# Two read-back loads moved up in a DMA queue and the last output store divided, in a gated FFT-filter kernel

## The chip, the core and the metric

The kernel runs on one core of a Trainium2 chip. A core has a matrix engine (PE, whose weight loads are listed apart as PEld), a vector engine (DVE), a scalar engine (ACT), a general engine (POOL) and a queue engine (SP) that does no arithmetic and issues the transfers; the transfers themselves run on the core's 16 DMA engines. The metric is the device time of one execution in microseconds (us); lower is better. The kernel before takes 117.5 us (median of 11 runs).

## What is computed

One input `x` of shape (1, 2048, 1024) goes through two Fourier filters that differ only in their weights, and the two results are mixed row by row with a gate:

```python
g = sigmoid((x * gate_w).sum(-1, keepdims=True))
def filt(x, w_r, w_i):
    X = rfft2(x.astype(float32), axes=(-2, -1)) * (w_r + 1j * w_i)
    return irfft2(X, s=(2048, 1024), axes=(-2, -1)).astype(bfloat16)
a, b = filt(x, A_w_r, A_w_i), filt(x, B_w_r, B_w_i)
return g * a + (1 - g) * b          # 2048 x 1024, bfloat16
```

## The kernel before, in words

The transforms are matrix products with cosine and sine tables. Columns of the spectrum are split into an even and an odd half (called parity 0 and 1); rows are split as 2048 = 128 x 16. The forward half of the kernel (tokens `F1`, `F2`, `F3`) brings the input to the spectrum, DVE multiplies the spectrum with both sets of weights (`P`, L494), and the first inverse stage (`J`, L537) works on 16 blocks: blocks 0 to 7 are the even parity, 8 to 15 the odd one.

Between the first inverse stage and the last two, the data changes its layout by a round trip through DRAM. A block's result is copied from PSUM to an `rl` tile (`R`, L204 on ACT or L206 on DVE), and two stores of 256 KB a block carry it to a scratch tensor `sc` (`H:block:half`, L549). Once all stores of a parity are there, eight loads of 512 KB bring it back (`L:parity:pair`, L554), the even parity into the tile `re` and the odd one into `ro`; a *pair* is two of the 16 row groups. Every load of a parity reads from all of its stores, so the first odd load `L:1:0` cannot be issued before the last odd store `H:15:0` has landed. Stores and loads are all issued by SP, in one queue. The kernel was given eight semaphores for the transfers of that queue, taken in turn, so each transfer is issued only when the eighth one before it has landed.

From the loaded pair PE computes the second inverse stage (`V:parity:pair:s`, L565: eight 128x128 products, s is the row of the pair), ACT or DVE copies the result to a `V` tile, and PE computes the last stage: `C` for the even parity (L590), `U` (L581) or `C` for the odd one. Even results are kept in `re` as sums and differences (`EX` copies them from PSUM, `EQ` on POOL, L615, adds and subtracts; `E` is a direct copy). Odd results are combined with the even ones into the output tile `ot` of the pair: `OR:pair:s:h` on DVE straight from PSUM (L635; h = 0 is the sum and the first half row, h = 1 the difference and the second half row), `OP` on POOL (L631) from a copy `OC`, and `QD` on DVE with `QP` on POOL (L642, L647) for pair 3. `S:S:pair` or `S:S:pair:s` stores both rows or one row of a finished pair (L652); a row in `ot` is 1024 elements of bfloat16, so a pair's tile is 512 KB and a row of it 256 KB. `ot` tiles share their five buffers with `rl` tiles.

The order of all this is written by hand: the string `ORDER` is a list of tokens, each token calls one function of `gated_mix`, and the instructions stand on every engine in just this order. No scheduler moves them. The last token of `V`, `C`, `U`, `F1` and so on is the PSUM bank; a letter A, D, P or S is the engine.

Around the change the even loads stand like this in `ORDER`: `L:0:0` to `L:0:4` early, then `L:0:5` after the stores `H:12:0` and `H:10:1`, then the nine stores `H:11:0`, `H:13:0`, `H:11:1`, `H:12:1`, `H:14:1`, `H:13:1`, `H:14:0`, `H:15:1`, `H:15:0`, then `L:0:6`, `L:0:7`, and then the odd loads `L:1:0` to `L:1:7`. PE uses them in the order of the tokens: `V:0:6` and `V:0:7` after the even pair 5, and `V:1:0` after them. The work ends with pair 6: four `OR` of it on DVE, of which the last three are the last three instructions of DVE, and one store `S:S:6` of the whole pair.

Of the kernel before, what the change touches and what calls it, by code (L numbers as in the profile page):

```python
# [10 lines left out]
P = 128  # L11
S = 2048
D = 1024
# [8 lines left out]


ORDER = """
warm:8 c:A:F1 c:A:gws tab:A x:S:0:1 x:S:1:1 x:S:2:2 x:S:4:2 x:S:6:2 x:S:8:2 x:S:10:2 x:S:12:2 x:S:14:2 c:S:FD:0:1
F1:1:o:0 F1:1:e:1 FX:1:o:D F1:0:o:2 FC:1:e:D F1:0:e:3 FP:1:o FD:1:e F1:3:o:0 F1:2:e:4 FC:0:e:D F1:3:e:1 gc:P FD:0:e
F1:2:o:5 FC:3:e:A FC:2:e:D F1:4:e:3 FD:3:e FX:2:o:A F1:5:o:6 FX:0:o:A FD:2:e F1:5:e:5 FC:4:e:A FP:0:o FX:3:o:A FD:4:e
F1:6:e:1 FC:5:e:A F1:4:o:2 FD:5:e FC:6:e:A F1:7:e:0 FP:2:o c:S:WF:0:4 FD:6:e F1:6:o:3 W:S:0 FC:7:e:A F1:9:e:7 FD:7:e
FX:6:o:A F1:8:e:1 FP:3:o FC:9:e:D c:S:WJ:0:4 F1:11:e:3 FD:9:e F1:10:e:0 c:S:w0 FC:11:e:A F1:7:o:4 c:S:PM FC:8:e:A
FP:6:o FD:11:e FX:5:o:A c:S:EZ F1:13:e:5 FC:10:e:A FD:8:e W:S:1 F1:12:e:6 FP:5:o FD:10:e c:S:WF:4:16 FC:12:e:A  # L30
F1:14:e:1 FC:13:e:A FD:12:e FX:4:o:A F1:15:e:3 W:S:2 F1:15:o:0 FD:13:e FP:4:o FC:15:e:A F1:11:o:2 FC:14:e:A FD:15:e
FC:15:o:A F1:8:o:6 c:S:WJ:4:16 F1:14:o:5 FD:14:e FC:8:o:A F1:10:o:3 neg:A:0:4 FD:15:o FC:14:o:A F1:12:o:7 FX:7:o:A
F2:0:0:1 FD:8:o c:S:E FC:10:o:A FP:7:o FC:12:o:A F2:1:0:0 W:S:3 FD:14:o T:0:0:A F2:0:1:4 FC:11:o:A F2:1:1:6 FD:10:o
T:1:0:A W:S:4 pw:P F1:13:o:1 T:1:1:A FD:12:o F1:9:o:0 T:0:1:A F3:1:5 FD:11:o c:S:FD:1:2 FC:9:o:A F3:0:3 FC:13:o:A
FD:9:o X:1:A W:S:5 F2:3:1:2 FD:13:o F2:2:0:7 X:0:A F2:3:0:0 P:1:0 W:S:6 Y:1:1 F2:2:1:5 T:3:0:A Y:0:3 neg:A:4:16 GH:4
P:1:1 W:S:7 T:2:0:A T:2:1:A NA:1:D N:1:D P:0:0 T:3:1:A GC:A NA:0:D P:0:1 F3:2:0 F2:4:0:5 X:2:A F2:4:1:2 F3:3:6 J:1:3:0
T:4:0:D T:4:1:A X:3:A P:2:0 Y:2:2 GT:0:5 R:1:0:A F2:5:0:6 Y:3:7 NA:2:D P:2:1 T:5:0:A H:1:0 F3:4:2 c:S:IG R:1:1:A
GT:1:5 W:S:8 F2:5:1:4 N:0:D NA:3:D P:3:0 X:4:A J:0:6:0 W:S:9 T:5:1:A H:1:1 N:2:D GT:2:5 P:3:1 R:0:0:A Y:4:2 GT:3:5
F3:5:3 W:S:10 R:0:1:A N:3:D H:0:0 F2:7:1:6 GK:D NA:4:D P:4:0 F2:6:1:2 X:5:A GZ:0:0 F2:6:0:5 P:4:1 GS:0 W:S:11 F2:7:0:7
T:7:0:A T:7:1:D J:2:3:0 T:6:0:A GW:D:4 T:6:1:A Y:5:6 GW:D:0 R:2:0:A N:4:D NA:5:D P:5:0 R:2:1:A H:2:0 W:S:12 H:0:1  # L40
P:5:1 F3:7:6 J:3:2:4 X:7:A H:2:1 F3:6:0 R:3:0:A F2:8:0:6 X:6:D F2:8:1:7 R:3:1:A F2:9:0:2 Y:7:3 T:8:0:D Y:6:0 T:8:1:A
GZ:1:4 NA:6:D T:9:0:A P:7:0 J:4:6:0 GS:1 F2:9:1:2 N:5:D P:7:1 R:4:0:A T:9:1:A H:4:0 P:6:0 J:5:4:6 W:S:13 R:4:1:A H:3:0
NA:7:D N:7:D R:5:0:A H:4:1 P:6:1 F3:8:2 F3:9:0 R:5:1:A F2:11:1:4 X:8:D F2:10:0:5 X:9:A H:5:1 F2:10:1:6 H:3:1 N:6:D
F2:11:0:7 W:S:14 P:8:0 T:10:0:A J:6:2:0 T:11:0:A T:11:1:A T:10:1:D R:6:0:A P:8:1 J:7:4:6 R:6:1:A H:6:0 F3:10:2 H:5:0
P:9:0 R:7:0:A P:9:1 R:7:1:A H:7:0 J:8:0:4 X:10:A GW:D:12 H:7:1 F2:12:0:6 H:6:1 F2:12:1:7 W:S:15 R:8:0:A T:12:0:D
P:10:0 R:8:1:A J:9:2:0 P:10:1 T:12:1:A H:8:1 F3:11:4 H:8:0 R:9:0:A F2:13:1:6 X:11:D R:9:1:A H:9:0 F3:12:2 F2:14:0:7
X:12:A H:9:1 F2:13:0:0 L:0:0 F2:14:1:1 L:0:1 T:13:0:A T:13:1:D P:11:0 L:0:2 J:10:4:2 L:0:3 T:14:0:A P:11:1 T:14:1:A
F3:13:6 R:10:0:A P:12:0 X:13:A H:10:0 J:11:0:4 L:0:4 P:12:1 R:10:1:A F3:14:6 R:11:0:A X:14:D F2:15:0:2 F2:15:1:3
T:15:0:A P:13:0 T:15:1:A J:12:0:6 R:11:1:A V:0:0:1:2 P:13:1 R:12:0:A F3:15:4 V:0:0:0:3 R:12:1:D X:15:A H:12:0
V:0:1:0:0 H:10:1 V:0:1:1:1 L:0:5 VC:0:1:0:A P:14:0 H:11:0 J:13:4:6 VC:0:0:0:A VC:0:1:1:A P:14:1 VC:0:0:1:A R:13:0:A  # L50
P:15:0 J:14:0:2 R:13:1:A H:13:0 H:11:1 C:0:0:1:4 P:15:1 H:12:1 C:0:0:0:5 EX:0:0:D R:14:0:D R:14:1:A EX:0:1:A H:14:1
J:15:6:2 H:13:1 EQ:0:1:0:P V:0:2:0:4 EQ:0:0:0:P C:0:1:1:5 R:15:0:D R:15:1:A H:14:0 C:0:1:0:0 EQ:0:0:1:P H:15:1
V:0:2:1:1 VC:0:2:0:A GW:D:8 V:0:3:1:2 H:15:0 EX:1:1:A L:0:6 V:0:3:0:3 VC:0:2:1:A EX:1:0:D L:0:7 EQ:1:1:0:P C:0:2:0:4
VC:0:3:0:D VC:0:3:1:A C:0:2:1:1 EQ:1:0:0:P V:0:4:1:0 EX:2:1:D EQ:0:1:1:P V:0:4:0:5 C:0:3:0:2 EQ:2:1:0:P VC:0:4:0:A
C:0:3:1:1 EX:2:0:A V:0:5:0:3 EQ:1:1:1:P VC:0:4:1:A V:0:5:1:5 EQ:1:0:1:P VC:0:5:0:A C:0:4:0:4 VC:0:5:1:A EQ:2:0:0:P
L:1:0 C:0:5:0:0 EX:4:0:D L:1:1 C:0:4:1:3 L:1:2 E:3:0:D EQ:4:0:0:P L:1:3 V:0:6:0:5 EX:4:1:A L:1:4 C:0:5:1:4 L:1:5
EQ:2:0:1:P VC:0:6:0:D V:0:6:1:2 L:1:6 EX:5:0:D EQ:4:0:1:P V:0:7:1:3 VC:0:6:1:A V:0:7:0:5 EX:5:1:A EQ:5:0:0:P C:0:6:0:0
L:1:7 C:0:6:1:2 EQ:2:1:1:P EX:6:1:A EQ:5:1:0:P VC:0:7:0:A VC:0:7:1:D E:3:1:D C:0:7:1:3 V:1:0:0:1 V:1:0:1:4 EQ:4:1:0:P
VC:1:0:0:A C:0:7:0:2 VC:1:0:1:D EX:6:0:A EQ:6:1:0:P U:1:0:0:1 EX:7:0:A EQ:6:1:1:P V:1:1:0:0 OC:0:0:A EQ:5:0:1:P
V:1:1:1:2 VC:1:1:0:D U:1:0:1:4 EQ:6:0:0:P V:1:2:0:5 EQ:7:0:0:P V:1:2:1:0 VC:1:2:0:A EQ:7:0:1:P U:1:1:0:1 VC:1:2:1:D  # L60
VC:1:1:1:A EQ:4:1:1:P EX:7:1:A U:1:2:0:5 OP:0:0:0 OR:0:1:1 OC:1:0:A OR:0:1:0 U:1:1:1:0 OR:2:0:0 EQ:6:0:1:P V:1:3:0:1
U:1:2:1:4 OP:0:0:1 VC:1:3:0:A V:1:3:1:2 V:1:4:0:1 OP:1:0:0 OR:1:1:0 OR:2:0:1 OR:2:1:1 S:S:0 VC:1:3:1:A OR:1:1:1
C:1:3:0:3 VC:1:4:0:A V:1:4:1:5 OR:2:1:0 EQ:7:1:0:P C:1:3:1:0 VC:1:4:1:A QD:3:0:0 S:S:2 U:1:4:0:1 OP:1:0:1 QD:3:1:1
V:1:5:0:2 QD:3:1:0 OC:4:0:A V:1:5:1:4 EQ:5:1:1:P S:S:1 VC:1:5:0:A QD:3:0:1 U:1:4:1:5 OP:4:0:0 VC:1:5:1:D U:1:5:0:0
OR:4:1:0 OP:4:0:1 U:1:5:1:1 OR:5:0:0 OR:4:1:1 V:1:7:0:4 QP:3:0:0:P V:1:6:1:2 OR:5:0:1 S:S:4 VC:1:7:0:A V:1:7:1:3
OR:5:1:1 U:1:7:0:4 VC:1:7:1:A EQ:7:1:1:P OR:5:1:0 V:1:6:0:0 QP:3:1:1:P OR:7:0:0 S:S:5 U:1:7:1:1 VC:1:6:0:A OR:7:0:1
VC:1:6:1:A QP:3:1:0:P U:1:6:0:0 S:S:7:0 OR:7:1:1 OR:7:1:0 U:1:6:1:2 QP:3:0:1:P OR:6:0:0 S:S:7:1 OR:6:1:1 OR:6:0:1
S:S:3 OR:6:1:0 S:S:6
"""


# [115 lines left out]
def gated_mix(ctx, tc, x_in, we_in, wo_in, w0_in, gw_in, out):  # L187
# [4 lines left out]
    ov = out.flatten_outer_dims().rearrange("(s2 s1) d -> s2 s1 d", s1=NS1)  # L192
# [7 lines left out]
    Q = {"S": nc.sync, "P": nc.gpsimd, "A": nc.scalar, "D": nc.vector}  # L200
# [19 lines left out]
    x = Re[:].rearrange("p (s d) -> p s d", s=NS1)  # L220
# [6 lines left out]
    C = {}  # L227
# [7 lines left out]
    warm = C["EA"][:].rearrange("p a b -> p (a b)")[:, 0:512]  # L235
    C["w0"] = C["EB"][:].rearrange("p a b -> p (a b)")[:, 1152:1408].rearrange("p (s u r t a w) -> p s u r t a w", s=2, u=NU, r=2, t=2, a=2)
    cnt = [0, 0]
    Ts, Xs, Ps, RLs, Vs, Ws, PS, TM, OT = {}, {}, {}, {}, {}, {}, {}, {}, {}
# [407 lines left out]
        t = TM["Q", v][:, h].rearrange("p s (g d) -> p s g d", g=2)  # L646
        Q[e].tensor_tensor(otile(v)[:, :, h, 256 * g:256 * g + 256], t[:, :, 0], t[:, :, 1], (ALU.add, ALU.subtract)[g])  # L647

    def store(q, v, s="b"):
        v = int(v)  # L650
        r = slice(0, 2) if s == "b" else slice(int(s), int(s) + 1)
        Q[q].dma_start(ov[:, 2 * v:2 * v + 2, :][:, r], OT[v][:, r].rearrange("p s h d -> p s (h d)"))  # L652

    fn = dict(warm=warmup, x=load_x, c=load_c, W=load_w, neg=neg, gc=gate_coef, tab=table, pw=pair_weights,
              F1=f1, FG=f1g, FY=f1y, FC=f1c, FD=f1d, FX=f1x, FP=f1p, GH=gate_hat, GC=gate_copy, GT=gate_turn, GK=gate_cols, GZ=gate_z, GS=gate_s, GW=gate_weights,
              F2=f2, T=f2c, F3=f3, X=f3c, P=prod, Y=parts, NA=patch_mul, N=patch, J=i1, R=i1c, H=scratch_store, L=scratch_load, V=i2, VC=i2c, U=i3, C=i3f,
              E=even_out, ES=even_sin, EF=even_sum, EX=even_parts, EQ=even_mix, OC=odd_copy, OP=odd_pool, OR=odd_row, QD=odd_mix, QP=odd_out, S=store)
    order = [tok.split(":") for tok in ORDER.split()]
    for t in order:
# [53 lines left out]
```

## Time and profile before

| what | value |
|---|---|
| median of 11 runs (lowest to highest) | 117.5 us (117.11 to 118.22) |
| the profiled execution's own time | 115.97 us |
| its span, first to last instruction | 114.2 us |
| PE busy | 102.7 us (90%) |
| DVE busy | 96.9 us (85%) |
| ACT busy | 84.5 us (74%) |
| POOL busy | 46.2 us (40%) |
| moved by DMA over the span | 36.79 MB, mean 322 GB/s |
| granted PE clock, mean | 0.995 of full speed |

Times inside the profile count from the first instruction of the span. "SPq" is SP issuing a transfer: the time beside it is that of the issue, not of the transfer, whose landing is given separately as time from issue to landing. In the chain of waits each piece was released by the piece before it; "issue" is time in which nothing that the profile shows was waited for. Because one execution is profiled, a difference of time is read inside it and then added to the median.

### The profile page before, as it was taken

Reading aid. Unit: us, or ns where it says so; the run is one execution under the profiler, and the core shown is the slowest. Engines: PE = TensorE matmul, PEld = TensorE weight load, DVE = VectorE, ACT = ScalarE, POOL = GpSimd, SP = SyncE. Lnnn points to the kernel's source line nnn. Section 1 sums busy time; section 2 is a strip of 40 time slices with the busy share of each in tenths; the row PEclk is TensorE's granted clock in tenths of the full one; section 3 lists DMA queues with packets and bytes.
Section 4 is the critical chain, followed back from the end, with each engine's and each line's share of the span. In section 5 each row is a group of like instructions: output and inputs, shape, how many; then the busy total and the mean of one; then the engine's idle time right before and its main releaser. Section 6 shows DMA issues by size and latency. Waiting matters only on the chain.

```text
span 114.2 us, 3953 instructions
## 1 busy us (share of the span) xinstructions
PE 102.7 (90%) x1619; PEld 70.7 (62%) x1619; DVE 96.9 (85%) x164; ACT 84.5 (74%) x138; POOL 46.2 (40%) x74
## 2 busy tenths in 40 slices
PE   5999999999999699897889899989999999999900
PEld 2599889775567356473445457459979666857400
DVE  0199999999999999999899999999266449999970
ACT  4018678999999999999999999977646753534300
POOL 1087994900000000000000000047988999999910
PEclk9999999999999999999999999999999999999998
DMA  3999999999488999579999999999999996583874
GB/s 92 369 354 413 396 363 369 353 412 420 189 253 292 362 397 396 165 223 395 377 330 370 302 349 394 290 366 381 351 354 321 354 416 245 225 326 135 323 277 184
DMA packets 17794, 36.79 MB, mean 322 GB/s; under 512 B 1904, under 2 KB 10736, under 8 KB 17776
## 3 DMA queue, kind: packets, MB, share of 16 engines
q1 hardware_dynamic: 17488, 36.44, 88.3%
q8 instruction: 12, 0.20, 0.7%
q10 hardware_dynamic: 288, 0.10, 0.5%
q14 instruction: 6, 0.05, 0.1%
HBM read 23.96 MB, written 12.58 MB: 320 GB/s over the span
## 4 chain that ended last, share of the span: by engine, by line
PE 33%; DMA 25%; DVE 18%; ACT 13%; issue 6%; SPq 1%; DVEq 1%; ACTq 0%
DMA re<-in_x_dram 9%; PE ps L581 9%; DVE p L494 9%; ACT rl L204 8%; PE ps L565 8%; DMA re<-sc 5%; DMA sc<-rl 4%; PE ps L334 4%; PE ps L450 4%; DMA ig<-cst_ig 4%; DMA gws<-in_gw_dram 3%; ACT X L204 3%; PE ps L590 3%; ACT T L204 2%; DVE ot L635 2%
## 5 line engine op out<-in xcount | busy, mean ns | idle before, releaser
L615 POOL TENSOR_TENSOR re<-wx 128x256 f32<-128x256 f32 x28 | 19.6, 730 | 54.7 <-DMA sc<-rl 53.2
L204 ACT CAST rl<-ps 128x1024 bf16<-128x1024 f32 x29 | 29.7, 1145 | 0.7 <-PE ps L537 0.7
L204 ACT COPY wx<-ps 128x256 f32<-128x256 f32 (+1 forms) x39 | 17.2, 500 | 9.7 <-PE ps L334 6.7
L537 PE MATMUL ps<-p,wj 32*64 32x512 bf16 x512 | 20.5, 381 | 2.5 <-ACT rl L204 2.0
L204 ACT CAST V<-ps 128x512 bf16<-128x512 f32 x25 | 13.8, 603 | 10.6 <-PE ps L565 7.7
L494 DVE TENSOR_TENSOR p<-X,ro 128x2048 bf16<-128x2048 bf16 x16 | 19.2, 1218 | 0.0
L450 PE MATMUL ps<-fd,y 128*128 128x256 bf16 x128 | 16.5, 273 | 0.5 <-ACT rl L204 0.4
L382 DVE TENSOR_TENSOR y<-ps,wx 128x256 bf16<-128x256 f32 x48 | 16.5, 420 | 0.1
L334 PE MATMUL ps<-f,re 128*128 128x128 bf16 x256 | 15.3, 219 | 0.5 <-DMA re<-in_x_dram 0.5
L204 ACT CAST T<-ps 128x512 bf16<-128x512 f32 x26 | 15.5, 696 | 0.0
L334 PEld LDWEIGHTS <-re 128*128 128x128 bf16 x256 | 14.5, 98 | 1.6 <-DMA re<-in_x_dram 1.2
L537 PEld LDWEIGHTS <-wj 32*64 32x64 bf16 x512 | 8.4, 103 | 10.7 <-issue 7.5
L382 POOL TENSOR_TENSOR y<-wx 128x256 bf16<-128x256 f32 x16 | 11.1, 729 | 7.4 <-DVE wx L206 5.2
L635 DVE TENSOR_TENSOR ot<-re,ps 128x512 bf16<-128x512 f32 x22 | 13.8, 682 | 0.4
L450 PEld LDWEIGHTS <-y 128*128 128x128 bf16 x128 | 11.6, 97 | 4.1 <-issue 2.8
L581 PE MATMUL ps<-ig,V 128*128 128x512 bf16 x56 | 13.4, 379 | 0.0
L204 ACT CAST X<-ps 128x1024 bf16<-128x1024 f32 x12 | 13.2, 1121 | 0.0
L206 DVE COPY wx<-ps 128x512 f32<-128x512 f32 (+1 forms) x10 | 5.7, 579 | 6.7 <-PE ps L334 4.2
L480 PE MATMUL ps<-T,wf 64*64 64x256 bf16 (+1 forms) x128 | 10.2, 332 | 1.1 <-DVE np L514 0.9
L590 PE MATMUL ps<-ig,V 128*128 128x256 bf16 x72 | 9.7, 273 | 0.0
L494 DVE TENSOR_TENSOR p<-X,wx 128x2048 bf16<-128x2048 bf16 x8 | 9.4, 1218 | 0.0
L494 DVE TENSOR_TENSOR p<-X,y 128x2048 bf16<-128x2048 bf16 x8 | 9.3, 1220 | 0.0
(60 smaller groups left out, 138.1 us busy)
## 6 DMA issues: line engine op xcount, KB each, us to landing
sc<-rl SPq DMA_DIRECT2D x32, 256.0 KB, 4.9
ro<-in_we_dram SPq DMA_DIRECT2D x8, 512.0 KB, 7.7
re<-sc SPq DMA_DIRECT2D x8, 512.0 KB, 6.0
ro<-sc SPq DMA_DIRECT2D x8, 512.0 KB, 7.2
re<-in_x_dram SPq DMA_DIRECT2D x7, 512.0 KB, 7.6
out_dram<-ot SPq DMA_DIRECT2D x7, 512.0 KB, 2.6
wx<-in_wo_dram SPq DMA_DIRECT2D x4, 512.0 KB, 7.2
y<-in_wo_dram SPq DMA_DIRECT2D x4, 512.0 KB, 5.2
```

The source lines that it names most:

```text
L204: nc.scalar.copy(out=out, in_=in_)
L334: nc.tensor.matmul(o, lhsT=lh, rhs=rh, start=(h == 0), stop=(h == 1))
L382: Q[e].tensor_tensor(yo[:, v, k:k + n, s1, :], a.rearrange("p (k c) -> p k c", c=4), b.rearrange("p (k c) -> p k c", c=4), op)
L450: nc.tensor.matmul(ps[:, v * 256:v * 256 + 256], lhsT=y[:, v, par, b, 2 * t:2 * t + 2, :, :].rearrange("p j s c -> p (j s c)"), rhs=C["FD" ...
L480: nc.tensor.matmul(view(ps[ho, tt * 512:(tt + 1) * 512], dst), lhsT=lh, rhs=view(T[hp(jh), tt, :], src), start=(w == 0), stop=(w == 1))
L494: nc.vector.tensor_tensor(p[:, r], xb, w, ALU.mult)
L537: nc.tensor.matmul(o, lhsT=lh, rhs=src[r, ri, wi, tt], start=(q == 0), stop=(q == 3))
L565: nc.tensor.matmul(ps[:, ch * 128:ch * 128 + 128], lhsT=RR[par][:, v, ch // 2, s, c0 + 256 * ab:c0 + 256 * ab + 128], rhs=Ew[:, s1, :], st ...
L581: nc.tensor.matmul(ps, lhsT=Vs[par, v][:, s, ch, :], rhs=rh, start=(ch == 0), stop=(ch == 3))
L590: nc.tensor.matmul(ps[:, o:o + 256], lhsT=Vs[par, v][:, s, ch, :], rhs=g[:, o:o + 256], start=(ch % 2 == 0), stop=(ch % 2 == 1))
L615: Q[e].tensor_tensor(EV[:, v, s, 256 * h:256 * h + 256], t[:, 0], t[:, 1], (ALU.add, ALU.subtract)[h])
L635: nc.vector.tensor_tensor(otile(v)[:, s, h, :], EV[:, v, s], PS["O", 1, v, s], (ALU.add, ALU.subtract)[h])
```

## The change

Two places of `ORDER` change, and `store` gets a fourth argument. Much of the string is also wrapped anew, which does nothing; the lines that hold moved tokens are these:

```diff
-V:0:1:0:0 H:10:1 V:0:1:1:1 L:0:5 VC:0:1:0:A P:14:0 H:11:0 J:13:4:6 VC:0:0:0:A VC:0:1:1:A P:14:1 VC:0:0:1:A R:13:0:A
-P:15:0 J:14:0:2 R:13:1:A H:13:0 H:11:1 C:0:0:1:4 P:15:1 H:12:1 C:0:0:0:5 EX:0:0:D R:14:0:D R:14:1:A EX:0:1:A H:14:1
...
-V:0:2:1:1 VC:0:2:0:A GW:D:8 V:0:3:1:2 H:15:0 EX:1:1:A L:0:6 V:0:3:0:3 VC:0:2:1:A EX:1:0:D L:0:7 EQ:1:1:0:P C:0:2:0:4
...
+V:0:1:1:1 L:0:5 L:0:6 VC:0:1:0:A P:14:0 H:11:0 J:13:4:6 VC:0:0:0:A VC:0:1:1:A P:14:1 VC:0:0:1:A R:13:0:A
+P:15:0 J:14:0:2 R:13:1:A H:13:0 L:0:7 H:11:1 C:0:0:1:4 P:15:1 H:12:1 C:0:0:0:5 EX:0:0:D R:14:0:D
...
+C:0:1:0:0 EQ:0:0:1:P H:15:1 V:0:2:1:1 VC:0:2:0:A GW:D:8 V:0:3:1:2 H:15:0 EX:1:1:A V:0:3:0:3 VC:0:2:1:A EX:1:0:D
...
-VC:1:6:1:A QP:3:1:0:P U:1:6:0:0 S:S:7:0 OR:7:1:1 OR:7:1:0 U:1:6:1:2 QP:3:0:1:P OR:6:0:0 S:S:7:1 OR:6:1:1 OR:6:0:1
-S:S:3 OR:6:1:0 S:S:6
+VC:1:6:1:A QP:3:1:0:P U:1:6:0:0 S:S:7:0 OR:7:1:1 OR:7:1:0 U:1:6:1:2 QP:3:0:1:P OR:6:0:0 S:S:7:1 S:S:3 OR:6:0:1
+S:S:6:0 OR:6:1:1 S:S:6:1:1 OR:6:1:0 S:S:6:1:0
...
-    def store(q, v, s="b"):
+    def store(q, v, s="b", h="b"):
         v = int(v)
         r = slice(0, 2) if s == "b" else slice(int(s), int(s) + 1)
-        Q[q].dma_start(ov[:, 2 * v:2 * v + 2, :][:, r], OT[v][:, r].rearrange("p s h d -> p s (h d)"))
+        o = ov[:, 2 * v:2 * v + 2, :][:, r].rearrange("p s (h d) -> p s h d", h=2)
+        if h == "b":
+            Q[q].dma_start(o.rearrange("p s h d -> p s (h d)"), OT[v][:, r].rearrange("p s h d -> p s (h d)"))
+        else:
+            Q[q].dma_start(o[:, :, int(h)], OT[v][:, r, int(h)])
```

In SP's queue the load `L:0:6` now stands right after `L:0:5`, ahead of nine stores of the odd parity, and `L:0:7` stands after `H:13:0`, ahead of seven of them. The last two rows of pair 6 are stored in three transfers instead of one: row 0 (256 KB) when `OR:6:0:1` is done, the second half of row 1 (128 KB) after `OR:6:1:1`, the first half of row 1 (128 KB) after `OR:6:1:0`. For that `OR:6:0:1` comes before `OR:6:1:1` on DVE. The streams of PE, ACT and POOL keep every instruction in its place.

## The prediction, made before the changed kernel was run

> **What bounds the kernel now.** I read the chain of waits first, from 79 us on.
>
> ```profile
> 79.03 5.16 DMA re<-sc
> 84.18 0.05 issue
> 84.23 0.62 PE ps L565 x8
> ...
> 106.01 0.88 PE ps L581 x4
> 106.89 0.03 issue
> 106.92 0.02 DVEq L635
> 106.94 0.04 issue
> 106.98 0.12 DVE ot L635
> ...
> 109.47 1.19 DVE ot L635 x2
> ```
>
> The first column is the start, the second the length. One even load (`L:0:6`) releases PE at 84.23, from there the chain is PE without a break to 106.89, and DVE's last `OR` end at 110.66. The last store follows. Then I read the busy time in stretches of 2 us around the loads, to see whether PE or the transfers have room there (PE, PEld, DVE, ACT, POOL busy; granted clock; DMA share; GB/s):
>
> ```profile
> 78.00:80.00 2.00, 2.00 (x32) 1.91 (x30) 1.81 (x4) 1.35 (x3) 1.46 (x3) 1.00 1.09 381
> 82.00:84.00 2.00, 2.00 (x23) 1.42 (x20) 0.88 (x2) 1.46 (x3) 1.69 (x4) 1.00 1.02 395
> 84.00:86.00 2.00, 1.84 (x29) 1.73 (x29) 1.46 (x3) 0.77 (x2) 2.00 (x3) 1.00 0.99 336
> 86.00:88.00 2.00, 2.00 (x29) 1.86 (x27) 1.53 (x3) 1.30 (x3) 1.62 (x3) 1.00 1.05 309
> ```
>
> PE idles 0.16 us in all, just before 84.23; the DMA engines are full throughout. So the wait for `L:0:6` that the chain shows is real, and only 0.16 us long. Next the queue of SP, one issue at a time in narrow windows, and PE's first product on odd data:
>
> ```profile
> 78.35 0.62 SPq L549 DMA_DIRECT2D sc<-rl  x1
> 79.03 0.96 SPq L554 DMA_DIRECT2D re<-sc  x1
> 80.03 0.50 SPq L554 DMA_DIRECT2D re<-sc  x1
> 82.94 0.32 SPq L554 DMA_DIRECT2D ro<-sc  x1
> 87.77 0.22 PE L565 MATMUL ps<-ea,ro 128*128 128x128 bf16 x1
> ```
>
> These are `H:15:0`, `L:0:6`, `L:0:7`, `L:1:0` and the start of `V:1:0`. From the view of transfers, with the last column the time from issue to landing, for the last three of the four transfers:
>
> ```profile
> re<-sc SPq DMA_DIRECT2D x1, 512.0 KB, 5.2
> re<-sc SPq DMA_DIRECT2D x1, 512.0 KB, 5.4
> ro<-sc SPq DMA_DIRECT2D x1, 512.0 KB, 4.1
> ```
>
> `H:15:0` takes 4.4, so it lands at 82.75, and SP, which waited for it, issues `L:1:0` 0.2 us later. While `L:1:0` starts up, `L:0:6` and `L:0:7` still keep the DMA engines full until 85.4. It lands at 87.0, 0.75 us before PE needs it. That cover is what the change moves.
>
> **Part 1, the two loads go up.** It removes at most PE's 0.16 us at 84.23. SP issues nothing more; `L:0:6` is moved past nine stores and `L:0:7` past seven, at 0.4 to 0.6 us an issue, in an order that keeps a backlog: stores near there take 4.4 us to land, so an issue 0.5 or 1 us later is hidden by that queue, and if the queue ran dry each would cost its own length. By the rule of eight in flight `H:14:0` now waits for the landing of `L:0:6` near 77.6, which still puts it in the queue 5 us ahead of its turn. Nothing on another engine waits for these stores soon: the five `rl` buffers are next written as `ot` at 93.55, eight us after the latest landing. What does wait for all of them is `L:1:0`. The transfers between the landing of `L:0:5` (70.50 issued, 5.8 to land: 76.3) and that of `L:0:7` (85.4) stay the same nine stores and two loads, 3.41 MB. So the *last* of them, now `H:15:0`, lands where `L:0:7` did: 85.4 if the 9.1 us stay, 84.9 if all went at 395 GB/s (8.6 us). I take 85.2, 2.45 us later than now. `L:1:0` is issued at 85.4, and nothing is in the queue ahead of it.
>
> How long does such a load take from an empty queue? The trace has no odd load like it, so bounds. Below, the 512 KB output stores from an idle queue land after 2.6 us. Above, the load of `y` at 46.77, behind one store of 256 KB, took 5.0. Nearest is the start of the program, also a read of DRAM with nothing ahead: 256 KB issued at 0.72 took 3.1, and 256 KB more at 395 GB/s make 3.8. I take 3.8, since a read is the same kind of work: `L:1:0` lands at 89.2, and with the 0.05 us between landing and PE seen at 84.18, `V:1:0` starts at 89.25 instead of 87.77: 1.45 us late (ends: 87.7 and no delay, even 0.15 gained, with 84.9 and 2.6; 90.65, a delay of 2.9, with 85.4 and 5.0). The next loads follow at 1.3 us each, and PE takes about 1.75 to 2.3 us a pair, so the first wait covers theirs.
>
> Is this delay won back? From `V:1:0` on PE has no gap up to the end of its products, and DVE's 27 instructions from 93.55 to 110.66 go at 0.6 us each with less than 0.8 us of waits for PE between. Both are full, so all 1.45 us reach DVE's last `OR`: 112.1.
>
> **Part 2, the last store.** DVE keeps its number of instructions; `OR:6:0:1` and `OR:6:1:1` change places and both banks are filled by then, so nothing. SP gets two more issues of 0.33 us, hidden between `OR`s that come 0.6 apart. The transfers:
>
> ```profile
> out_dram<-ot SPq DMA_DIRECT2D x1, 256.0 KB, 2.0
> out_dram<-ot SPq DMA_DIRECT2D x1, 512.0 KB, 2.6
> ```
>
> 256 KB cost 0.57 us (2.04 against 2.61 by the records), so 128 KB alone would land after 1.75 (2.04 less half of 0.57) at the soonest, and after 2.04, like a store twice its size, at the latest. It saves 0.57 to 0.86 of the 2.61. But the queue is one: `S:S:3` (512 KB, waiting for POOL) is issued at 109.01 now, lands at 111.63, and 512 KB more behind it take 1.14, to 112.77. So without any delay the end comes at 112.44 to 112.8 instead of 113.30. With the delay: POOL's `OP` of pair 4 waits for an ACT copy that ended at 100.50, POOL started it at 100.87, so POOL is 1.1 us late, `S:S:3` issues at 110.1 and lands at 112.7, and the three stores of pair 6 land at 113.85 by the queue, 113.9 by the last one's own 1.75. I take 113.95, between that and 114.2.
>
> [...]
>
> **Sum.** 1.45 for the odd loads' late start, less 0.8 saved at the tail: 113.95 against 113.30, +0.65 in the profiled execution (115.97, span 114.2). That execution lies 1.5 below the median, so I add the difference to the median: 117.5 + 0.65 = 118.15, say 118.2.
>
> **The rivals.** First, faster: the start-up of `L:1:0` stays within the cover it has. If an idle-queue load lands in 2.6 us like an output store, and the stores land by 85.0, `V:1:0` starts at 87.8 or before; the 0.16 at 84.23 goes nowhere then, and the tail gives 0.5 to 0.86: 116.8. For it speaks that the output stores do land that fast; against it, that each read from a drained queue in this trace took over 3. It decides at 2.7 us from issue to landing.
>
> Second, a tie: a load in between, 2.9 to 3.3 us, delays PE by 0.4 to 0.9 and the tail pays for it: 117.5.
>
> Third, worse: the restart is slow for two loads. Now `L:1:1` lands 2.3 us after `L:1:0` (83.31 and 6.0: 89.3), so refilling an emptying queue already cost a load and a bit more, and the `y` load's 5.0 happened after a drain. Then the delay is 2.9, the tail gives 0.5: 119.9.
>
> That the change does not do what it says: the last store, though smaller, stays behind `S:S:3` if POOL comes later than I think, and saves only 0.4; then 118.5.
>
> **How the numbers follow.** Forecast, slower by 0.4 to 1.2 (117.9 to 118.7): 0.45. The worse case 0.10, the stuck store 0.05, all slower. Tie 0.17; faster 0.23. A run can tell about 0.3% (0.35 us) from no change. Slower by more: 0.60; within: 0.17; faster: 0.23. The range reaches from the upper part of the faster case, 116.9, to below the worst, 119.4; the likeliest case alone has 117.9 to 118.7.
>
> **What would show it.** `H:15:0` landing near 85 instead of 82.75; `L:1:0` issued near 85.4; a wait of PE for a load of `ro` before the first L565 on it, 1 us or more, in place of 0.16 for `re`; DVE's last `OR` ending 1 to 2 us later; the last store landing under 2.1 us after its issue. The prediction fails if `L:1:0` lands before 88, or if the odd part has room that I do not see, so that PE's delay is gone by 106.

## The result, and the profile after

| | median of all runs | lowest to highest | runs |
|---|---|---|---|
| before, beside it | 117.5 us | 116.34 to 118.77 | 47 |
| changed | 120.93 us | 119.47 to 123.39 | 12 |

The changed kernel is slower: ratio 1.0249, 95% interval [1.0208, 1.029]. I forecast slower, but by 0.65 us; it is 3.4 us, outside my range. The ratios here are formed without executions more than 1.5% above the fastest of the same kernel; some of the kernels below spread more than that by a mechanism of their own, so the medians and spreads over all runs stand beside the ratios.

The profiled execution took 120.23 us with a span of 118.4, 4.2 more than the one before. Its chain of waits in the part where the change lies (start, length, what):

```profile
80.99 5.86 DMA sc<-rl
...
87.07 3.60 DMA ro<-sc
90.67 0.05 issue
90.71 1.89 PE ps L571 x16
92.60 0.85 PE ps L596 x4
93.45 1.15 PE ps L587 x4
94.61 0.89 PE ps L571 x16
...
113.83 1.20 DVE ot L641 x2
```

Where the chain had an even load of 5.16 us and then PE without a break, it now has the last odd store, behind it the first odd load, and only then PE. (Lines moved by six: L571 is the second inverse stage, L596 and L587 the last one, L641 DVE's `OR`.) The products of PE on either side of that wait, from the timeline, with the idle time before them and its releaser in brackets:

```profile
87.74 0.49 PE L596 MATMUL ps<-ig,V 128*128 128x256 bf16 x3
90.71 0.29 PE L571 MATMUL ps<-ea,ro 128*128 128x128 bf16 x1 [2.48 <-DMA ro<-sc]
```

PE now waits 2.48 us for `L:1:0`. And the chain shows a second thing: sixteen products of L571 take 1.89 us at 90.71 and 0.89 at 94.61. The reason is in the busy times of three stretches of 3.41 us, cut where the granted clock changes (PE, PEld, DVE, ACT, POOL busy; clock; DMA share; GB/s):

```profile
87.09:90.50 3.41, 1.14 (x11) 0.78 (x8) 0.77 (x2) 1.17 (x3) 3.41 (x6) 1.00 0.69 221
90.50:93.91 3.41, 3.20 (x22) 2.59 (x23) 0.69 (x1) 1.44 (x3) 1.71 (x3) 0.50 1.03 422
93.91:97.33 3.42, 3.42 (x41) 2.49 (x40) 0.73 (x2) 1.25 (x3) 3.12 (x4) 1.00 1.02 413
```

For one stretch of 3.41 us PE is granted half its clock, just after the stretch in which it was mostly idle.

The two profiled executions differ as follows. Up to the end of the first inverse stage, about where the change begins, the later one is 0.63 us behind (the chain's three `rl` copies start at 72.89 instead of 72.26). `V:1:0` starts at 90.71 instead of 87.77: 2.94, of which 2.31 are new. From there to DVE's end it takes 24.31 us instead of 22.89: 1.42. From DVE's end to the end of the span 3.40 instead of 3.54: 0.14 saved. Together 0.63 + 2.31 + 1.42 - 0.14 = 4.22.

### The profile page after: what moved, and what is told of

It reads as the page before. It is cut to its first block, busy times and chain, and to the rows that moved or that the text cites. A ratio compares the mean times of both kernels' runs of the same rounds, so it can differ in the third digit from the quotient of the medians.

```text
span 118.4 us, 3958 instructions
## 1 busy us (share of the span) xinstructions
PE 104.7 (88%) x1619; PEld 72.0 (61%) x1619; DVE 97.1 (82%) x164; ACT 84.7 (72%) x138; POOL 46.3 (39%) x74
## 4 chain that ended last, share of the span: by engine, by line
PE 34%; DMA 23%; DVE 15%; ACT 15%; issue 7%; SPq 1%; DVEq 1%; ACTq 0%
PE ps L587 9%; DMA re<-in_x_dram 9%; PE ps L571 8%; DVE p L500 8%; ACT rl L210 8%; DMA sc<-rl 5%; PE ps L456 4%; PE ps L340 4%; ACT X L210 4%; DMA ig<-cst_ig 3%; DMA ro<-sc 3%; PE ps L596 3%; DMA f<-cst_f 3%; ACT T L210 2%; DVE ot L641 2%
## 5 line engine op out<-in xcount | busy, mean ns | idle before, releaser
L641 DVE TENSOR_TENSOR ot<-re,ps 128x512 bf16<-128x512 f32 x22 | 13.8, 683 | 0.4
L587 PE MATMUL ps<-ig,V 128*128 128x512 bf16 x56 | 13.8, 386 | 0.0
L212 DVE CAST V<-ps 128x512 bf16<-128x512 f32 x7 | 4.8, 691 | 8.3 <-ACT V L210 4.8
L571 PEld LDWEIGHTS <-ro 128*128 128x128 bf16 x128 | 8.5, 104 | 4.4 <-DMA ro<-sc 2.8
L571 PE MATMUL ps<-ea,ro 128*128 128x128 bf16 x64 | 8.9, 230 | 2.5 <-DMA ro<-sc 2.5
```

The lines of the kernel that those rows point to most:

```text
L212: Q[e].tensor_copy(out=out, in_=in_)
L571: nc.tensor.matmul(ps[:, ch * 128:ch * 128 + 128], lhsT=RR[par][:, v, ch // 2, s, c0 + 256 * ab:c0 + 256 * ab + 128], rhs=Ew[:, s1, :], st ...
L587: nc.tensor.matmul(ps, lhsT=Vs[par, v][:, s, ch, :], rhs=rh, start=(ch == 0), stop=(ch == 3))
L641: nc.vector.tensor_tensor(otile(v)[:, s, h, :], EV[:, v, s], PS["O", 1, v, s], (ALU.add, ALU.subtract)[h])
```

## The experiments

"Before" is the kernel before on the same chip in the same session.

| run | median (lowest to highest), runs | median of before | ratio [95%] |
|---|---|---|---|
| loads only | 120.05 (117.82 to 122.71), 12 | 117.39 | 1.0111 [1.0053, 1.0168] |
| tail only | 117.79 (116.98 to 118.78), 12 | 117.39 | 1.0031 [0.9987, 1.0074] |
| changed + 10 matmuls | 118.88 (118.69 to 122.22), 6 | 117.39 | 1.0161 [1.0103, 1.0218] |
| loads past two stores | 121.48 (119.24 to 123.6), 6 | 117.39 | 1.0257 [1.0175, 1.0338] |
| one load only | 117.54 (116.83 to 118.89), 12 | 117.28 | 1.0028 [0.9986, 1.007] |
| loads only + useless load | 120.06 (117.99 to 120.91), 6 | 117.28 | 1.0125 [1.0052, 1.0197] |
| tail, half rows by ACT | 116.96 (116.07 to 117.73), 12 | 117.28 | 0.9972 [0.994, 1.0003] |
| changed + 4 matmuls | 119.1 (118.64 to 120.02), 4 | 117.28 | 1.0167 [1.0108, 1.0227] |
| changed, again | 119.05 (118.35 to 121.81), 6 | 117.32 | 1.0139 [1.0077, 1.0201] |
| tail, whole row by ACT | 116.83 (115.94 to 117.43), 12 | 117.32 | 0.9991 [0.9953, 1.0029] |
| one load + half rows by ACT | 117.48 (116.68 to 118.8), 12 | 117.32 | 1.0009 [0.9969, 1.0049] |

### Which of the two parts

Loads only, on the kernel before (here and below the tokens of `ORDER` stand on lines of their own):

```diff
 L:0:5
+L:0:6
 VC:0:1:0:A P:14:0 H:11:0
...
 R:13:1:A H:13:0
+L:0:7
 H:11:1
...
 H:15:0 EX:1:1:A
-L:0:6
 V:0:3:0:3 VC:0:2:1:A EX:1:0:D
-L:0:7
 EQ:1:1:0:P
```

> Only the two loads are moved; the last pair is stored in one transfer as before. Theory (drained queue): nothing is left behind the last odd store, so the first odd load starts on an empty queue, lands 3.5 to 3.8 us after its issue, PE idles 2 to 2.5 us and then runs at about half clock for some 4 us: +3.4 to +3.9 us against before, i.e. the whole of the change's loss and 0.2 to 0.4 more, since the tail's saving is missing. Rival (the tail costs): the three small stores make part of the loss, then this run loses clearly less than the changed kernel, under +3.0 us.

Tail only, on the kernel before:

```diff
-OR:6:0:0 S:S:7:1 OR:6:1:1 OR:6:0:1 S:S:3 OR:6:1:0 S:S:6
+OR:6:0:0 S:S:7:1 S:S:3 OR:6:0:1 S:S:6:0 OR:6:1:1 S:S:6:1:1 OR:6:1:0 S:S:6:1:0
```

> Only the last store is divided; the loads stand as before. Theory: the three stores run behind the store of pair 3 in one queue, so they save 0.2 to 0.4 us (the changed kernel's trace has 2.4 us from DVE's end to the last landing instead of 2.6). What I predicted blind would be 0.5 to 0.8 us. Rival (the tail costs): +0.3 us or more.

The loads alone cost 2.7 us in the median, with a spread of 4.9 us; the tail alone moves nothing that the interval can tell (+0.4 us in the median). So the loss is the loads', and my 0.8 us at the tail are not there. (The 2.7 lie below the 3.0 under which I had expected the tail to share in the loss. But the tail alone costs nothing that can be told, and six further executions of the changed kernel, below, came out only 1.7 us above before: 0.7 us between two kernels that spread like this tell nothing.) In the tail run's profile DVE's end is followed by the last landing after 2.43 us, and by the end of the span after 3.44; before it was 2.64 and 3.54. The saving in the span is 0.1 us.

### How far up the loads go

Both loads past the last two stores only:

```diff
 H:14:0 C:0:1:0:0 EQ:0:0:1:P
+L:0:6 L:0:7
 H:15:1 V:0:2:1:1 VC:0:2:0:A GW:D:8 V:0:3:1:2 H:15:0 EX:1:1:A
-L:0:6
 V:0:3:0:3 VC:0:2:1:A EX:1:0:D
-L:0:7
 EQ:1:1:0:P
```

> Both loads go up past the last two stores only (behind H:14:0, ahead of H:15:1), one store at the end as before. Theory (drained queue): what counts is that no load stands behind the last store, not how far up the loads went; last store lands near 85.5, first odd load 3.5 to 3.8 us after its issue, PE idles about 2 us, +3.0 to +3.9 us. Rival (eight in flight: the loads high up make later stores wait for their landing, so the queue is issued late): here no store waits for these loads, and most of the loss is gone, under +1 us.

It is as slow as the changed kernel (+4.1 us). No store waits here for the landing of a moved load before it may be issued; it is enough that the last stores land behind the two loads. Last store landed at 86.78, first odd load issued at 86.98 and landed 3.55 later, PE idle 2.37 us. The rival, that most of the loss comes from eight in flight throttling the queue, falls.

One load only:

```diff
 L:0:5
+L:0:6
 VC:0:1:0:A P:14:0 H:11:0
...
 H:15:0 EX:1:1:A
-L:0:6
 V:0:3:0:3 VC:0:2:1:A EX:1:0:D L:0:7
```

> Only L:0:6 goes up behind L:0:5; L:0:7 stays behind the last store as cover of one load instead of two. Theory (cover): the first odd load is issued some 1.3 us later than before, but behind a load that still runs; it lands 4.0 to 4.5 us after its issue, PE idles 0.5 to 1.5 us, the clock stays at 1.0 in the odd part, and the loss is a part only: +0.4 to +1.4 us. Rival (any move of these loads costs the same, because the stores behind them come late): +2.5 us or more, as with both loads.

It loses nothing that can be told (1.0028 [0.9986, 1.007]). Issues of SP in its profile, and PE's first odd product; then the landing of the two transfers:

```profile
80.57 0.82 SPq L554 DMA_DIRECT2D re<-sc  x1
85.42 0.33 SPq L554 DMA_DIRECT2D ro<-sc  x1
88.90 0.23 PE L565 MATMUL ps<-ea,ro 128*128 128x128 bf16 x1
```

```profile
re<-sc SPq DMA_DIRECT2D x1, 512.0 KB, 5.9
ro<-sc SPq DMA_DIRECT2D x1, 512.0 KB, 3.4
```

The first odd load landed at 88.85 and PE started at 88.90, having idled 0.01 us. One load moved uses up the slack; the second is what costs. The expectation was 0.4 to 1.4 us of loss, so the price of the first was put too high: the load behind the last store did not slow the odd one, which took 3.4 us rather than 4.0 to 4.5.

### Is it the empty queue?

The loads-only kernel with a useless load:

```diff
+    def dummy_load(k):
+        k = int(k)
+        nc.sync.dma_start(yf[:, k, 1, 2048:4096], w_in[0][k])
...
 H:15:0
+DL:0
 EX:1:1:A V:0:3:0:3
```

> Both loads moved up, one store at the end, and one useless load of 512 KB from an input into an idle part of a tile is put behind the last odd store, so the queue is not empty when the first odd load is issued. Theory (cover): the first odd load lands about 1.3 us of useless transfer plus 1.6 us after the last store instead of 3.8 us, PE idles 0.5 to 1.2 us less than with the loads alone (1.76 us there in the profile), and the median falls by 0.5 to 1.5 us against e1 although 512 KB more are moved. Rival (the queue is only bound by its bytes): 1.3 us later than e1, about 121.3.

Neither came: 120.06 against 120.05. SP's issues of the useless load and of the first odd load, and their landing:

```profile
81.86 0.35 SPq L280 DMA_DIRECT2D y<-in_we_dram  x1
86.67 0.33 SPq L558 DMA_DIRECT2D ro<-sc  x1
```

```profile
y<-in_we_dram SPq DMA_DIRECT2D x1, 512.0 KB, 5.9
ro<-sc SPq DMA_DIRECT2D x1, 512.0 KB, 3.8
```

The useless load landed at 87.77, 1.25 us after the last store, and the odd load 3.79 us after its issue all the same. So an empty queue is no slower than one with a load in it: a 512 KB load takes 3.4 to 3.8 us from its issue in all nine profiles in which at most one load ran ahead of it (3.43, 3.51, 3.55, 3.59, 3.60, 3.61, 3.62 and 3.71 without the useless load, 3.79 with it), and a load that runs during that time costs hardly anything (3.79 us here, 3.61 in the same kernel without it). In the kernel before both even loads run during that time, in the changed one none does. My picture of a queue that must not run dry was wrong in this; what counts is when the last store lands.

### Is it the clock?

On the changed kernel; the second variant has `warm:4:6` (each is a product of the row table `ea` with itself):

```diff
 C:0:7:1:3
+warm:10:6
 V:1:0:0:1
```

> The changed kernel with ten extra matmuls of 128x512 (2.2 us by 215 ns each) into an unused PSUM bank just before PE's first product on odd data; they leave the result as it is. PE then does not idle while it waits for the load. Theory (the idle PE loses its clock): granted clock 1.0 in 90 to 94 us, sixteen V products in 0.9 us instead of 1.9, and 1.4 to 1.9 us faster than the changed kernel, about 119.2. Rival (the clock has other causes, or the slow products have): the clock still falls to 0.5 to 0.6 and the time stays within 0.4 us of the changed kernel or is worse.

> The changed kernel with four instead of ten extra matmuls (0.9 us) ahead of the first product on odd data, so PE idles about 1.6 us instead of 2.5. If the clock falls after an idle stretch longer than some 2 us, it stays at 1.0 here in the profile and the time is within 0.5 us of the run with ten, about 119. If any idle above 0.6 us does it, the low clock is there for 3.4 us, and the time is 1.4 us or more above it.

The extra matmuls write a PSUM bank that is not in use there and change no result. By the medians, extra work on PE, put where it waits, takes 1.6 us off: 118.94 is the median of the ten runs with extra matmuls, 120.51 that of all eighteen runs of the changed kernel. Alone this is weak, since the first twelve of these eighteen have a median of 120.93 and the six further ones, below, 119.05.

The granted clock says more. It is on record for each execution as a mean over its span, and one stretch of 3.41 us at half clock takes 0.014 off it. In the 129 such executions of the kernel before and of the variants with at most one load moved it is never below 0.985, so a lower one is a sign of such a stretch. With both loads moved and no extra matmuls it is below 0.985 in 24 of 42 executions (the changed kernel alone: 10 of 18), with extra matmuls in one of ten, which is also the slowest of them (122.22 us). The ten of the changed kernel below 0.985 have a median of 121.49 us, the other eight 119.67. So the matmuls make the low clock rarer, not impossible.

In both profiles the odd part runs from `V:1:0` to DVE's end in 22.79 us, as before (22.89), and the clock stays at 1.00. With four matmuls PE idled 2.24 us, not the expected 1.6, since the load came later, and the clock held nonetheless. So a bound on the idle time does not decide. I cut the profiles into stretches of 3.41 us, on the grid on which the clock changes in the same trace. The first number after the length is PE's busy time in the stretch, the third from the end the clock. For the stretch with the wait and the next one, loads only:

```profile
87.09:90.50 3.41, 1.65 (x22) 1.31 (x21) 0.48 (x1) 1.16 (x3) 3.41 (x7) 1.00 0.94 335
90.50:93.91 3.41, 3.41 (x38) 2.33 (x35) 1.38 (x2) 2.06 (x4) 3.05 (x6) 1.00 1.02 417
```

The useless load:

```profile
86.50:89.91 3.41, 1.66 (x19) 1.27 (x16) 1.29 (x2) 1.69 (x4) 3.37 (x6) 1.00 0.66 219
89.91:93.32 3.41, 2.77 (x34) 2.22 (x36) 0.69 (x1) 1.97 (x4) 2.48 (x5) 1.00 1.03 419
```

Ten extra matmuls (the stretch with the wait only), then four:

```profile
87.80:91.21 3.41, 2.77 (x18) 1.29 (x16) 0.06 (x1) 1.07 (x2) 3.41 (x6) 1.00 0.83 280
```

```profile
87.57:90.98 3.41, 2.15 (x16) 1.35 (x14) 0.97 (x2) 1.37 (x3) 3.41 (x6) 1.00 0.41 125
90.98:94.39 3.41, 2.37 (x27) 1.77 (x28) 0.69 (x1) 1.56 (x3) 1.72 (x3) 1.00 1.03 413
```

Loads past two stores:

```profile
88.17:91.58 3.41, 1.04 (x18) 1.01 (x18) 0.00 (x0) 1.07 (x3) 3.29 (x5) 1.00 0.90 345
91.58:94.99 3.41, 3.41 (x21) 2.12 (x18) 0.69 (x1) 1.94 (x4) 2.54 (x4) 0.50 1.03 420
```

After the ten the clock stays at 1.00 as well. With 1.65 us or more of work in a stretch the next one runs at full clock, with 1.14 or less at half. In the run with the useless load PE idled 2.34 us in one piece, almost the 2.37 of the last one, but the boundary at 89.91 cut it in two.

### The spread

> The changed kernel once more, beside the two below on one chip. The clock is read off windows of 3.41 us that start at a different point of each execution: in the profiles so far a window with 2.27 or 2.37 us of PE idle was followed by one at half clock, one with 1.76 us or less was not. So executions of this kernel, with about 2.5 us of idle, fall into groups, with the low window and without, some 1.5 us apart: a spread of 3 us or more from lowest to highest, median +3 to +4 us, where the kernels without the moved loads spread by 2 us. If the spread is a matter of the day, it is as narrow as theirs.

The spread came (3.5 us here, 3.9 in the twelve runs above, 1.8 to 2.4 in the four sets of before), the median did not: 119.05. Three of its six runs are at 118.35 to 118.6, as the runs with extra matmuls, and the two at 121.5 and 121.8 are 3 us higher, twice the 1.5 us that I had expected between the groups. The intervals of the two sets, [1.0208, 1.029] and [1.0077, 1.0201], do not even overlap, although the kernel is the same: with groups like these, an interval from a few executions is too narrow. Its profile is one of the high ones:

```profile
88.25:91.66 3.41, 0.40 (x4) 0.11 (x2) 0.03 (x1) 1.07 (x2) 3.41 (x6) 1.00 0.65 208
91.66:95.07 3.41, 3.00 (x22) 2.48 (x23) 0.69 (x1) 1.24 (x3) 0.97 (x2) 0.50 1.01 389
```

Here the last store landed at 88.21, PE idled 3.42 us instead of 2.48, and the next stretch is at half clock again: from `V:1:0` to DVE's end it takes 24.21 us. So in this profile the wait and the clock each make a part of the extra time, and the clock's 1.4 us are not the whole distance between the groups.

### The tail

Two variants of the tail-only kernel; `S:A` is a store issued by ACT, in its own queue, instead of SP. Half rows by ACT:

```diff
-S:S:6:0 OR:6:1:1 S:S:6:1:1 OR:6:1:0 S:S:6:1:0
+S:S:6:0 OR:6:1:1 S:A:6:1:1 OR:6:1:0 S:A:6:1:0
```

The whole row by ACT:

```diff
-S:S:6:0 OR:6:1:1 S:S:6:1:1 OR:6:1:0 S:S:6:1:0
+S:S:6:0 OR:6:1:1 OR:6:1:0 S:A:6:1
```

> Loads as before; the last pair is stored as row 0 from SP's queue and the two half rows of row 1 from ACT's queue. If the half rows are late because they stand behind the store of pair 3 in SP's queue, they land about 2.0 us after DVE's end instead of 2.4, and the time is 0.3 to 0.5 us under before. If the transfers themselves share the same engines, the order of issue does not matter and it is as e2, within 0.15 us.

> Loads as before; the last pair as row 0 from SP's queue and the whole of row 1 (256 KB) from ACT's queue after DVE's last instruction. If the transfers of the last 1 MB simply follow each other behind the store of pair 3 at 0.65 us for 256 KB, halving row 1 gains nothing, and the last landing is 2.3 to 2.5 us after DVE's end, -0.2 to -0.4 us against before. If a half row really lands sooner, this is 0.2 us or more behind the run with half rows in ACT's queue.

From DVE's end to the last landing it takes 2.48 us with half rows by ACT and 2.35 with the whole row, against 2.64 before. Halving the row gains nothing. Why shows in the landings of the last four stores of the changed kernel, by issue and by time to landing:

```profile
113.12 0.34 SPq L660 DMA_DIRECT2D out_dram<-ot  x1
113.85 0.33 SPq L660 DMA_DIRECT2D out_dram<-ot  x1
114.45 0.52 SPq L662 DMA_DIRECT2D out_dram<-ot  x1
115.06 0.59 SPq L662 DMA_DIRECT2D out_dram<-ot  x1
```

```profile
out_dram<-ot SPq DMA_DIRECT2D x1, 512.0 KB, 2.9
out_dram<-ot SPq DMA_DIRECT2D x1, 256.0 KB, 2.8
out_dram<-ot SPq DMA_DIRECT2D x1, 128.0 KB, 2.6
out_dram<-ot SPq DMA_DIRECT2D x1, 128.0 KB, 2.4
```

They land at 116.00, 116.66, 117.04 and 117.42: back to back, 0.66 us for 256 KB and 0.38 for each 128 KB, behind pair 3, which waited for POOL. Pair 3's store in its turn landed 1.29 us behind the second row of pair 7 (114.71), the pace of the two after it: it was issued 1.90 us before DVE's end instead of 1.65 in the kernel before, and landed 0.98 us after it instead of 0.97. So the earlier issue of pair 3 gained nothing, and the smaller last stores 0.24 us (from DVE's end to the last landing 2.40 instead of 2.64). Either variant by ACT has the lowest medians of this study, 0.3 and 0.5 us under before, but both intervals hold 1, so neither is shown to beat it.

> What lost nothing, together: L:0:6 moved up, L:0:7 left behind the last store, row 0 from SP's queue and the two half rows from ACT's queue. Theory: L:0:6 takes away PE's wait of 0.16 to 0.5 us for it and the first odd load comes just in time, so with the tail's 0.3 us -0.2 to -0.6 us against before. Rival (the one load moved uses up all the slack): +0.2 us or more in the median, with some executions a microsecond slower.

Its edit is the one-load edit and the half rows by ACT together. At 117.48 against 117.32 it is neither: PE idled 0.14 us in the profile, the slack is used up, and some executions pay for it (up to 118.8).

## Why the prediction was right and wrong, by its own steps

**What `L:1:0` waits for: right.** The last odd store took the place of `L:0:7` as the last transfer, the odd load's issue moved behind it, and nothing of the delay was won back: from `V:1:0` on, profiles without a low clock take 22.8 to 22.9 us to DVE's end, as before.

Together the sum forecast 0.65 us, and the profile, less the 0.63 of the part ahead of the change, has 3.59. Of the 2.94 us between them 0.86 are the later start of `V:1:0`, 1.42 the clock and 0.66 the tail. Without the clock 2.17 would be left, so the clock is the step that was missing, and two terms were sized wrong besides.

**The landing of the last store: size off by 1 us.** I put it 2.45 us later. It is 86.85, less the 0.63 that the execution was behind anyway: 3.5 later than 82.73. From the landing of `L:0:5` on it is 8.66 us, as I worked out (8.6 to 9.1), but `L:0:5` itself landed later, 1.65 us after the start of the last product of the first inverse stage (L537) instead of 0.43. In the six profiles in which neither or only one of the two loads moves that number is 0.01 to 0.78, in the seven with both moved 0.59 to 2.28. Part of it was there before the change could act: the store just ahead of `L:0:5` in the queue, issued before either moved load, landed 0.12 us before the start of that product instead of 0.81, which is 0.7 of the 1.2 us. No run here tells the rest, and that stays open. Counted from that product's start, the last odd store lands after 6.66 to 6.96 us with no load moved (four profiles), 8.39 and 8.72 with one, and 9.58 to 11.25 with both (seven).

**The odd load from an empty queue: right in size, wrong in reason.** I took 3.8 us, between the bounds 2.6 and 5.0; it is 3.60, and 3.55 to 3.61 in the others with both loads moved and no extra work. The reason I gave, start-up from an empty queue, is wrong by the useless load: the load took 3.79 us with another one in the queue.

**"`V:1:0` starts 1.45 us late": 2.31.** (My terms add up to 1.48.) This is the store's extra microsecond, less 0.2 of the load.

**Nothing for the clock: the step that failed.** My sum carried PE's wait as time lost once. It is paid a second time, since one stretch of 3.41 us at half clock follows when the wait leaves a stretch with too little work: 1.42 us in this profile. That the low clock costs this is shown by the rows: sixteen products take 1.89 us instead of 0.89, and the odd part takes 24.21 to 24.44 us in the three profiles with such a stretch and 22.79 to 22.89 in the ten without. That the wait brings it about is shown by the extra matmuls: they fill the wait, bring no result, and the low clock comes in one of ten executions instead of 10 of 18. My list of rivals had no such case. Where the grid falls is luck: the six further executions alone, at 119.05, would have looked like a forecast that was only somewhat too low.

**The tail: 0.8 us saved forecast, 0.14 measured.** I priced the small store by its own landing and saw the store of pair 3 ahead of it, but with 0.57 us for 256 KB, the difference of two stores that stood alone. Back to back it is 0.66, and the half rows 0.38 each. By those the last landing is 1.42 us behind pair 3's instead of 1.14, and so the queue sets the end by itself. That is 0.28 us; about as much again is pair 3's own store, which I let land 0.6 us after DVE's end and which landed 0.98 after it, since it stood back to back behind pair 7's second row and took 2.88 us instead of 2.62. The case in which the last store stays stuck behind pair 3's came true in kind, with less saved than its 0.4.

**The rivals.** The faster one needed 2.7 us for the odd load; no profile is below 3.4. The worse one, 119.9, came nearest in size, with the wrong cause: the second odd load followed the first by 1.2 to 1.8 us, not slowly.

## What to carry to other kernels

Where one transfer may only start once all of a group have landed, put transfers that are independent of it behind the group, not ahead: they run in the latency that follows anyway, and moving them up moves the group's end by their full length, 1.3 us each here at 395 GB/s. (In the profiles the end moved by more, some 1.8 us with one load and 3.6 with two; the part above the full length stays unexplained.) Price a wait of a busy matrix engine twice, the wait itself and a possible stretch at half clock after it, and look at the granted clock before explaining a spread. A smaller last store pays little if something of size stands right before it in the same transfer engines (0.24 us to the last landing here).

## What the runs showed of the hardware

The granted clock of PE changes on a fixed grid of 3.41 us whose start differs from one execution to the next: in the changed kernel's trace it changes at 90.50, 93.92 and 117.81, which are 1 and 7 steps apart, and in every trace here its changes lie whole steps apart. In seven profiles the stretch after the wait was at 0.50 when the one with the wait had 0.40, 1.04 or 1.14 us of PE work in it, and at 1.00 with 1.65, 1.66, 2.15 and 2.77. The ends of the executions, where PE runs out of work, agree: the stretch after one with 0.11 to 1.37 us of work was at 0.50 (seven profiles), after one with 2.01 to 2.64 us at 1.00 (five). So the boundary in these runs lies between 1.37 and 1.65 us. The Trainium skill (*TensorE: Matmul & The Clock Gate*, "Part 1: The HAM clock gate") describes such a free-running window of 3413 ns, which agrees, and says that the clock falls after at least one idle window of about 3.4 us. The runs did not need a window that is idle throughout: waits of 2.37 and 2.48 us, in windows a third busy, were enough.

The time of a kernel with such a wait therefore depends on where the grid falls and on how long the wait is in that execution, and a median over few runs can land anywhere between: 119.05 and 120.93 for the same kernel.
